# Spectral layer and two MLPs on one core: half sums and differences of the odd samples made by a negation and an in-place DMA add, with six x buffers and an earlier load

## Chip, core and metric

One core of one Trainium2 chip. The metric is the time of one execution on the device in microseconds, the median of the runs; lower is better. TensorE (PE) does the matrix products, VectorE (DVE), ScalarE (ACT) and GpSimd (POOL) the elementwise work, SyncE (SP) issues most DMAs; DMAs that add into their target are issued by GpSimd.

## What is computed

A spectral layer on x (2 batches, 3008 samples, 256 features), and two MLPs of width 2048 on its result. The change is in the forward transform of x.

```python
X = np.fft.rfft(x, axis=1)
Yr = Xr @ w_r - Xi @ w_i + b_r
Yi = Xr @ w_i + Xi @ w_r + b_i
Y = soft_threshold(Yr, 0.01) + 1j * soft_threshold(Yi, 0.01)
y = np.fft.irfft(Y, n=3008, axis=1)          # (2, 3008, 256)
h = y.reshape(6016, 256) @ w_in;  g = h * sigmoid(1.702 * h);  x1 = g @ w_out
h = x1 @ w_in2;                   g = h * sigmoid(h);          out = g @ w_out2
```

## The kernel before

The transform of 3008 samples is folded before TensorE sees it: samples are sorted into even (q = 0) and odd (q = 1), and of each kind the four that a symmetry ties together lie side by side in one row, so a tile `raw` has 128 rows of 4 x 256 numbers: two halves of 512 columns. A kind and batch (q, b) has three such tiles (j = 0, 1, 2). From each tile come the sum and the difference of its two halves (`halves`, line 313: 128x512 each; cs = 0 is the sum, cs = 1 the difference). For the even samples they are kept (`keep`) for use much later, for the odd ones they lie in `lv`. From these, `fold` makes the sum or difference of their own two 256-column halves (line 332, tile `xf`; for some of the odd ones first `dd` and then a second sum and difference of two `dd`, line 346). The `xf` tiles are the stationary operands of TensorE, which multiplies them with cosine and sine matrices (`m0`, loaded by `load_m`) into PSUM (`psf`); ScalarE copies the result out (line 446).

The forward stage works through 16 groups in one written order: groups 0 to 3 are the even samples of batches 0 and 1 (line 428, `fwd_pair`, two at a time), groups 4 to 7 the odd samples of batch 0 (t = 0 to 3), groups 8 to 11 the odd samples of batch 1, groups 12 to 15 the even samples again with other matrices (line 394, `fwd_mm`). t % 2 picks the half sums (t = 0, 2) or the half differences (t = 1, 3). In the loop over groups, `fold` runs three groups ahead of the products. A group of t < 2 has eight products of 190 columns; each product stands in the trace as two matmul records. The first product of such a group needs the first tile, the second product already the third tile.

Every engine runs its instructions in the written order (a region in which the scheduler is told to keep it), and SP and GpSimd issue their DMAs in that order too: an issue that waits holds up the ones behind it. Loads of x are issued on SP by `load_raw`; `raw` has three buffers, so a fourth tile waits until VectorE has read the first; the second batch's even x goes to other buffers (`xr`). `load_m` has four buffers, so the fifth matrix waits until TensorE is done with the first. After the forward transform, weights of the MLPs are converted in steps that are spread over the stages (lines 180 to 190: ScalarE, five VectorE operations, and a GpSimd DMA that adds in place, `cv_a<-cv_c`); the first such step stands on VectorE behind the folds of group 9.

Of the kernel before, what the change touches and what calls it, by code (L numbers as in the profile page):

```python
# [9 lines left out]
F32 = mybir.dt.float32  # L10
# [7 lines left out]
ALU = mybir.AluOpType  # L18

B, S, D, FF = 2, 3008, 256, 2048  # L20
HALF = S // 2
P = 128
NJ = 3
# [5 lines left out]
MW = 2 * NJ * CW  # L29
# [10 lines left out]
def split_sums(kind, q, p):  # L40
    return (kind, q) == ("f", 0) and CFG.get("eo", "1111")[p] == "1" or (kind, p) == ("i", 0) and CFG.get("eo", "1111")[2 + q] == "1"


def mshape(kind, q, p):
    if split_sums(kind, q, p):
        return 4, {("f", 0, 0): 190, ("f", 0, 1): 188, ("i", 0, 0): 192, ("i", 1, 0): 188}[kind, q, p]
    return {("f", 0, 0): (3, 380), ("f", 0, 1): (3, 376), ("f", 1, 0): (4, 190), ("f", 1, 1): (3, 376), ("i", 0, 0): (3, 378), ("i", 1, 0): (3, 376), ("i", 0, 1): (4, 190), ("i", 1, 1): (3, 376)}[kind, q, p]
# [9 lines left out]
def spectral_mlp_kernel(ctx, tc, xin, mfwd, minv, wc, bias, w_in1, w_out1, w_in2, w_out2, outT):  # L57
    nc = tc.nc
# [3 lines left out]
    def N(k):  # L62
        return CFG.get(k, NUM[k])

    def E(site, i=0):
        s = CFG.get(site, DEF[site])
        return {"V": nc.vector, "P": nc.gpsimd}[s[i % len(s)]]
# [15 lines left out]
    def opened(name, side=None, bufs=1, **kw):  # L83
        ex[name] = ExitStack()
        return ex[name].enter_context(tc.tile_pool(name=name, bufs=bufs, side=side, reuse_waits="tile", **kw))
# [5 lines left out]
    m_p = opened("m", "left", 4)  # L91
# [7 lines left out]
    def bank(i, name):  # L99
        return ps_p[i % 2].tile([P, 512], F32, tag="ps", name=name)  # L100
# [14 lines left out]
    def slot(cls, dtype, name):  # L115
        return xt_p.tile([P, 2 * D], dtype, tag=f"x{cls}", name=name, bufs=14 if cls == 0 else 12)
# [4 lines left out]
    def load_m():  # L121
        if not m_order:
            return
        kind, q, t = key = m_order.pop(0)
        nb, w = mshape(kind, q, t // 2)
        if kind == "f":
            m = m0_p.tile([P, NJ * 380], F32, tag="m0", name="m0")[:, : nb * w]
            m_tiles[key] = m.rearrange("p (j c) -> p j c", j=nb)
            src = mfwd[t // 2, q, t % 2][:, : nb * w]
            if key[1:] in ((0, 0), (0, 1)):  # L130
                return m_tiles[key], src.rearrange("p (j c) -> p j c", j=nb)
            nc.sync.dma_start(out=m, in_=src)
            return
        m = m_p.tile([P, MW], F32, tag="m", name="m")
        for cs in range(2):
            mc = m[:, cs * MW // 2 : cs * MW // 2 + nb * w]
            nc.sync.dma_start(out=mc, in_=minv[t // 2, q, cs][:, : nb * w])
            m_tiles[kind, q, t + cs] = mc.rearrange("p (j c) -> p j c", j=nb)
# [128 lines left out]
    def tick(k=1):  # L267
        window(k, settle(True))
        pump()
        cv_load(1 - len(loaded))  # L270
# [6 lines left out]
    region('fwd')  # L277

    m0_p = opened("m0", "left", 4)
    raw_p = opened("raw", "left", 3)  # L280
    lv_p = opened('lv', 'left', N('lvb'))
    xs_p = opened("xs", "left", 18)
    groups = [(0, b, cs) for b in range(B) for cs in range(2)]
    groups += [(1, b, t) for b in range(B) for t in range(4)]
# [1 line left out]
    held, kept = [], []  # L286
    raws, lvs, xs = {}, {}, {}
    raw_units = [(q, b, j) for q in range(2) for b in range(B) for j in range(NJ)]

    def load_raw(k=1):  # L290
        for _ in range(min(k, len(raw_units))):
            u = q, b, j = raw_units.pop(0)
            if (q, b) == (0, 1):
                raws[u] = [slot(h, F32, "xr")[:, :].rearrange("p (k d) -> p k d", k=2) for h in range(2)]
                for h in range(2):
                    nc.sync.dma_start(out=raws[u][h], in_=xin[q, b, j][:, 2 * h : 2 * h + 2])
                continue
            t = raw_p.tile([P, 4, D], F32, tag="raw", name="raw")
            raws[u] = t[:, 0:2], t[:, 2:4]
            nc.sync.dma_start(out=t, in_=xin[q, b, j])  # L300

    def halves(q, b, j, cs):
        if q == 0:
            if len(held) % 4 == 0:
                kept.append(m_p.tile([P, MW], F32, tag="m", name="keep"))
            k = len(held) % 4
            lv = kept[-1][:, k * 2 * D : (k + 1) * 2 * D].rearrange("p (k d) -> p k d", k=2)
            held.append(lv)
        else:
            lv = lv_p.tile([P, 2, D], F32, tag="lv", name="lv")  # L310
        lvs[q, b, cs, j] = lv
        r = raws[q, b, j]
        (nc.vector.tensor_sub if cs else nc.vector.tensor_add)(lv, *r)  # L313

    def fold(g):
        if g >= len(groups):
            return
        q, b, t = groups[g]

        cs, minus = t % 2, t in (1, 2)  # L320
        pair = []
        for j in range(NJ):
            if t == 0:
                halves(q, b, j, 0)
            lv = lvs[q, b, cs, j]
            e = E('dd', t * NJ + j) if g >= 2 else E('dd0', t * NJ + j)
            paired = q == 1 and t < 2 and j < 2
            if paired:
                xf = lv_p.tile([P, D], F32, tag="dd", name="dd", bufs=4)
            else:  # L330
                xf = xs_p.tile([P, D], F32, tag="xh", name="xf")
            (e.tensor_sub if minus else e.tensor_add)(xf, lv[:, 0], lv[:, 1])  # L332
            if t == 0:
                halves(q, b, j, 1)
                del raws[q, b, j]
                if (q, b) == (0, 0):
                    load_raw()
            if not paired:
                xs[(*groups[g], j)] = (xf, None)
                continue  # L340
            pair.append(xf)
            if j == 1:
                for x in range(2):
                    e = E('pr', 2 * t + x)
                    xf = xs_p.tile([P, D], F32, tag="xh", name="xf")
                    (e.tensor_sub if x else e.tensor_add)(xf, pair[0], pair[1])
                    xs[(*groups[g], x)] = (xf, None)

    def fold_pair(g):
        q, b, _ = groups[g]  # L350
        for j in range(NJ):
            for cs in range(2):
                halves(q, b, j, cs)
                xf = xs_p.tile([P, D], F32, tag="xh", name="xf")
                lv = lvs[q, b, cs, j]
                (nc.vector.tensor_sub if cs else nc.vector.tensor_add)(xf, lv[:, 0], lv[:, 1])
                xs[q, b, cs, j] = (xf, None)
            del raws[q, b, j]
            if b == 0:
                load_raw()  # L360

    def load_wc():
        raws["wc"] = raw_p.tile([P, 4, D], F32, tag="raw", name="wc_f")
# [55 lines left out]
    def fwd_pair(g):  # L419
        out = {}  # L420
        for h in (g, g + 1):
            out[h] = [bank(h, "psf") for _ in range(2)]
        for j in range(NJ):
            for h in (g, g + 1):
                q, b, t = groups[h]
                w = mshape("f", q, t // 2)[1]
                for mm in range(2):
                    nc.tensor.matmul(out[h][mm][:, :w], xs[q, b, t, j][0][:, mm * P : (mm + 1) * P], m_tiles["f", q, t][:, j, :w], start=j == 0, stop=j == NJ - 1)
        return [(h, out[h]) for h in (g, g + 1)]
# [51 lines left out]
    for j in range(NJ):  # L481
        load_raw()
        for ms, src in first:
            for k in ((0,), (1,), (2, 3) if split_sums("f", 0, 0) else (2,))[j]:
                nc.sync.dma_start(out=ms[:, k], in_=src[:, k])
    load_raw(3)
    fold_pair(0)
    load_m()
    fold_pair(2)
    load_m()  # L490
    xsp, lo_p = {}, []
    mids = [(b, p, j) for b in range(B) for p in range(2) for j in range(NJ)]

# [14 lines left out]
            xsp[b, p, j, cs, part] = t[:, :].rearrange("p (q m c) -> p q m c", q=2, m=2)  # L508

    prev = fwd_pair(0)  # L510
    fold(4)
    then = fwd_pair(2)
    load_m()
    fold(5)
    load_raw(3)
    for x in prev:
        fwd_evac(*x)
    load_m()
    fold(6)
    new_xt(1)  # L520
    pads(1)
    cv_load(1)
    prev = then
    for g, (q, b, t) in enumerate(groups):
        if g < 4:
            continue
        ps = fwd_mm(g)
        if b == B - 1 and m_order[0][0] == "f":
            load_m()
        fold(g + N('fa'))  # L530
        for x in prev:
            fwd_evac(*x)
        prev = [(g, ps)]
        if g == 6:
            wc_s = m_p.tile([P, MW], F32, tag="m", name="wc_s")[:, : 6 * D].rearrange("p (k d) -> p k d", k=2)
            load_wc()
        if g == 8:
            prep_wc()
            lo_p.append(wc_p)
        if g == 10:  # L540
            xsplit(N('n32'), 1)
        if g in N('tf'):
            tick(N('tf').count(g))
# [249 lines left out]
    prev = None  # L793
    for q in range(2):
        for b in range(B):
            for t in range(4):
# [5 lines left out]
                prev = (q, b, t, ps)  # L802
# [171 lines left out]
    for at, (l, i, p) in enumerate(seq):  # L974
# [8 lines left out]
        k = rate(at)  # L983
# [182 lines left out]
```

## Time and profile before

| | |
|---|---|
| median of 3 runs | 1153.8 us (1153.64 to 1153.8) |
| the profiled execution: its own time | 1153.61 us |
| its span, first to last instruction | 1151.8 us |
| TensorE busy | 1141.4 us |
| VectorE, ScalarE, GpSimd busy | 629.9, 775.1, 476.2 us |
| mean granted TensorE clock | 0.999 |

The times of rows are microseconds from the span's start in this one execution. A TensorE that is shown busy is not one at its peak, since matmuls are pipelined and their ends are modelled; starts are exact.

### The profile page before, as it was taken

Reading aid. Unit: us, or ns where it says so; the run is one execution under the profiler, and the core shown is the slowest. Engines: PE = TensorE matmul, PEld = TensorE weight load, DVE = VectorE, ACT = ScalarE, POOL = GpSimd, SP = SyncE. Lnnn points to the kernel's source line nnn. Section 1 sums busy time; section 2 is a strip of 40 time slices with the busy share of each in tenths; the row PEclk is TensorE's granted clock in tenths of the full one; section 3 lists DMA queues with packets and bytes.
Section 4 is the critical chain, followed back from the end, with each engine's and each line's share of the span. In section 5 each row is a group of like instructions: output and inputs, shape, how many; then the busy total and the mean of one; then the engine's idle time right before and its main releaser. Section 6 shows DMA issues by size and latency. Waiting matters only on the chain.

```text
span 1151.8 us, 14646 instructions
## 1 busy us (share of the span) xinstructions
PE 1141.4 (99%) x5094; PEld 947.1 (82%) x5094; DVE 629.9 (55%) x1014; ACT 775.1 (67%) x1446; POOL 476.2 (41%) x411
## 2 busy tenths in 40 slices
PE   9999999999999999999999999999999999999998
PEld 6768987878888888888889878888888888888897
DVE  8888997765565475564564642532622623623422
ACT  2587367877677676686677776766766866756755
POOL 0253164453444434444447645433343333333333
PEclk9999999999999999999999999999999999999999
DMA  8699493531121212212111100010000100100000
GB/s 312 168 185 240 113 160 79 109 81 37 49 61 37 72 39 55 56 38 73 46 47 37 46 26 3 1 38 1 19 19 1 37 1 1 37 1 1 37 1 32
DMA packets 39996, 68.95 MB, mean 60 GB/s; under 512 B 3697, under 2 KB 16241, under 8 KB 39922
## 3 DMA queue, kind: packets, MB, share of 16 engines
q1 hardware_dynamic: 26306, 45.51, 12.0%
q0 software_dynamic: 13616, 22.51, 11.5%
q8 instruction: 40, 0.66, 0.2%
q14 instruction: 34, 0.28, 0.1%
HBM read 35.15 MB, written 10.35 MB: 40 GB/s over the span
## 4 chain that ended last, share of the span: by engine, by line
PE 91%; DVE 3%; ACT 3%; issue 2%; DMA 2%; POOL 0%; SPq 0%; DVEq 0%; POOLq 0%; ACTq 0%
PE o L843 41%; PE x L871 36%; PE psm L575 5%; PE psi L394 4%; PE psf L394 3%; PE psm L572 1%; ACT yt L874 1%; DMA xr<-in_x 1%; DVE yt L893 0%; ACT x L782 0%; DMA raw<-in_wi 0%; ACT g L876 0%; ACT yt L890 0%; DVE keep L313 0%; DMA raw<-in_x 0%
## 5 line engine op out<-in xcount | busy, mean ns | idle before, releaser
L881 POOL TENSOR_TENSOR g<-yt,g 128x512 fp32r<-128x512 f32 (+1 forms) x282 | 362.8, 1298 | 495.9 <-PE x L871 359.8
L843 PE MATMUL o<-g,wo 128*128 128x512 f32 (+1 forms) x2304 | 560.0, 385 | 0.6 <-DMA wo<-cv_a 0.6
L871 PE MATMUL x<-x,wi 128*128 128x512 f32 (+1 forms) x2016 | 499.0, 386 | 3.4 <-ACT yt L912 2.1
L843 PEld LDWEIGHTS o<-g,wo 128*128 128x128 f32 x2304 | 432.4, 188 | 81.6 <-DMA wo<-cv_a 1.0
L871 PEld LDWEIGHTS x<-x,wi 128*128 128x128 f32 x2016 | 377.1, 188 | 80.0 <-ACT yt L912 5.0
L874 ACT ACTIVATE yt<-yt 128x512 f32<-128x512 f32 (+1 forms) x288 | 179.0, 622 | 253.7 <-DVE yt L922 204.9
L876 ACT CAST g<-yt 128x512 fp32r<-128x512 f32 (+1 forms) x384 | 235.2, 612 | 12.3
L922 DVE TENSOR_TENSOR yt<-yt,x 128x512 f32<-128x512 f32 (+1 forms) x96 | 64.7, 674 | 214.5 <-PE x L871 213.9
L893 DVE TENSOR_TENSOR yt<-yt,x 128x512 f32<-128x512 f32 (+1 forms) x96 | 64.8, 676 | 167.2 <-ACT yt L890 165.3
L881 DVE TENSOR_TENSOR g<-yt,g 128x512 fp32r<-128x512 f32 (+1 forms) x102 | 70.1, 687 | 73.5 <-ACT g L876 73.5
L190 POOL DMA_DIRECT2D cv_a<-cv_c x32 | 28.0, 876 | 111.8 <-DVE cv_c L189 105.7
L926 DVE TENSOR_TENSOR yt<-yt,x 128x512 f32<-128x512 f32 (+1 forms) x96 | 64.8, 675 | 0.0
L789 DVE TENSOR_TENSOR x<-yt,x 128x512 fp32r<-128x512 f32 (+1 forms) x44 | 46.4, 1054 | 29.5 <-ACT x L782 29.5
L910 ACT COPY yt<-x 128x512 f32<-128x512 f32 (+1 forms) x96 | 54.8, 571 | 3.3 <-PE x L871 3.3
L874 ACT ACTIVATE yt<-x 128x512 f32<-128x512 f32 (+1 forms) x96 | 56.1, 585 | 0.0
L912 ACT COPY yt<-x 128x512 f32<-128x512 f32 (+1 forms) x96 | 55.7, 580 | 0.1
L890 ACT COPY yt<-x 128x512 f32<-128x512 f32 (+1 forms) x96 | 54.6, 569 | 0.0
L394 PE MATMUL psi<-m,f 128*128 128x188 f32 (+3 forms) x224 | 45.1, 357 | 0.0
L394 PEld LDWEIGHTS psi<-m,f 128*128 128x128 f32 x224 | 37.6, 190 | 5.7
L394 PE MATMUL psf<-m,xf 128*128 128x190 f32 (+2 forms) x176 | 36.2, 367 | 1.0 <-DVE xf L332 0.6
L394 PEld LDWEIGHTS psf<-m,xf 128*128 128x128 f32 x176 | 29.6, 190 | 8.0 <-ACT xt L446 1.0
L782 ACT CAST x<-tmp 128x512 fp32r<-128x512 f32 (+1 forms) x36 | 22.1, 614 | 17.1 <-DVE tmp L791 15.5
(116 smaller groups left out, 839.4 us busy)
## 6 DMA issues: line engine op xcount, KB each, us to landing
raw<-in_wi SPq DMA_DIRECT2D x32, 256.0 KB, 3.7
cv_a<-cv_c POOLq DMA_DIRECT2D x32, 256.0 KB, 5.1
raw<-in_wo SPq DMA_DIRECT2D x16, 512.0 KB, 3.8
xl<-xt POOLq DMA_DIRECT2D x20, 256.0 KB, 7.9
out_t<-yt SPq DMA_DIRECT2D x20, 256.0 KB, 2.0
raw<-in_x SPq DMA_DIRECT2D x9, 512.0 KB, 5.8
wi<-tmp POOLq DMA_DIRECT2D x8, 256.0 KB, 4.8
w_in<-cv_a SPq DMA_DIRECT2D x8, 256.0 KB, 2.0
```

Of the source, the lines that this page charges most:

```text
L394: nc.tensor.matmul(ps, hi[:, c : c + P], m[:, k, :w], start=i == 0, stop=i == last)
L575: nc.tensor.matmul(t, st, mv, start=n == 0 and k == 0, stop=n == 3 and grp == 1 and k == 2)
L843: nc.tensor.matmul(acc[h, mm], st, mv, start=first and k == 0, stop=last and k == 2)
L871: nc.tensor.matmul(ps, st, mv, start=first and m == 0, stop=m == 2, skip_group_check=True)
L874: nc.scalar.activation(g, g if src is None else src, func)
L876: nc.scalar.copy(gh, g)
L881: eng.tensor_sub(gl, g, r32(gh))
L893: nc.vector.tensor_add(y1, y1, Y)
L910: nc.scalar.copy(y2, Z)
L912: nc.scalar.copy(y3, X)
L922: nc.vector.tensor_add(y2, y2, X)
L926: nc.vector.tensor_add(y3, y3, Z)
```

## The change

For the odd samples the two results no longer lie in tiles of their own but replace the two halves of the x tile itself. `second(b)` lets ScalarE negate the second half r1 in place. In batch 0, VectorE then makes the sum as r0 - (-r1) in place, and a GpSimd DMA reads the first half once more from DRAM and adds it to the negated half, which makes the difference. In batch 1 both results come from DMAs: one adds the second half to r0, one the first half to the negated r1. So of the 12 VectorE operations (128x512) three remain, and there are six ScalarE operations and nine adding DMAs of 256 KB that were not there. The x tiles get six buffers in place of three, and the loads of the second batch's odd x stand in the SP queue ahead of the third and fourth matrix. Copies out of groups 0 and 1 stand ahead of `fold(4)` in the text.

```diff
-    raw_p = opened("raw", "left", 3)
-    lv_p = opened('lv', 'left', N('lvb'))
+    raw_p = opened("raw", "left", 6)
+    lv_p = opened('lv', 'left', 4)
...
     def halves(q, b, j, cs):
-        if q == 0:
-            if len(held) % 4 == 0:
-                kept.append(m_p.tile([P, MW], F32, tag="m", name="keep"))
...
-        else:
-            lv = lv_p.tile([P, 2, D], F32, tag="lv", name="lv")
...
+    def second(b):
+        for j in range(NJ):
+            r = lvs[1, b, 0, j], lvs[1, b, 1, j] = raws.pop((1, b, j))
+            nc.scalar.mul(r[1], r[1], -1.0)
+            if b == 1:
+                for h in range(2):
+                    nc.gpsimd.dma_start(out=r[h], in_=xin[1, b, j][:, 2 - 2 * h : 4 - 2 * h], accum_op=ALU.add)
 
     def fold(g):
...
-            if t == 0:
-                halves(q, b, j, 0)
             lv = lvs[q, b, cs, j]
+            if (q, b, t) == (1, 0, 0):
+                r = lvs[q, b, 1, j]
+                nc.vector.tensor_sub(lv, lv, r)
+                nc.gpsimd.dma_start(out=r, in_=xin[q, b, j][:, 0:2], accum_op=ALU.add)
...
-            if t == 0:
-                halves(q, b, j, 1)
-                del raws[q, b, j]
-                if (q, b) == (0, 0):
-                    load_raw()
...
             del raws[q, b, j]
-            if b == 0:
-                load_raw()
...
+    load_raw(6)
+    load_m()
+    load_m()
     load_raw(3)
     fold_pair(0)
-    load_m()
     fold_pair(2)
-    load_m()
...
     prev = fwd_pair(0)
+    for x in prev:
+        fwd_evac(*x)
+    second(0)
     fold(4)
     then = fwd_pair(2)
     load_m()
     fold(5)
-    load_raw(3)
-    for x in prev:
-        fwd_evac(*x)
...
         for x in prev:
             fwd_evac(*x)
+        if g == 4:
+            second(1)
```

How it moves instructions, on three engines. First VectorE, from behind the last fold of group 3 on: the rows of groups 4 and 5 before. `lv<-raw` is a half sum or difference, the wait names what a row waits for (DMAHW: a load of SP has landed; DMASW: a DMA of GpSimd has landed).

```order
L313 TENSOR_TENSOR lv<-raw 128x512 [waits DMAHW7_49]
L332 TENSOR_TENSOR dd<-lv 128x256 [waits DVE_49]
L313 TENSOR_TENSOR lv<-raw 128x512
L313 TENSOR_TENSOR lv<-raw 128x512 [waits DMAHW0_49]
L332 TENSOR_TENSOR dd<-lv 128x256 [waits DVE_49]
L313 TENSOR_TENSOR lv<-raw 128x512
L346 TENSOR_TENSOR xf<-dd 128x256 [waits DVE_49]
L346 TENSOR_TENSOR xf<-dd 128x256
L313 TENSOR_TENSOR lv<-raw 128x512 [waits DMAHW1_49]
L332 TENSOR_TENSOR xf<-lv 128x256 [waits DVE_49]
L313 TENSOR_TENSOR lv<-raw 128x512
L332 TENSOR_TENSOR dd<-lv 128x256 x2
```

And the same place in the change, from behind its first half sum (`raw<-raw`, in place) to the last fold of group 5:

```order
L339 TENSOR_TENSOR dd<-raw 128x256 [waits DVE_49]
L331 TENSOR_TENSOR raw<-raw 128x512 [waits DMAHW0_49,Activation_49]
L339 TENSOR_TENSOR dd<-raw 128x256 [waits DVE_49]
L348 TENSOR_TENSOR xf<-dd 128x256 [waits DVE_49]
L348 TENSOR_TENSOR xf<-dd 128x256
L331 TENSOR_TENSOR raw<-raw 128x512 [waits DMAHW1_49,Activation_49]
L339 TENSOR_TENSOR xf<-raw 128x256 [waits DVE_49]
L339 TENSOR_TENSOR dd<-raw 128x256 [waits DMASW0_49]
L339 TENSOR_TENSOR dd<-raw 128x256 [waits DMASW1_49]
L348 TENSOR_TENSOR xf<-dd 128x256 [waits DVE_49]
L348 TENSOR_TENSOR xf<-dd 128x256
L339 TENSOR_TENSOR xf<-raw 128x256 [waits DMASW2_49]
```

Three half differences are gone from among the folds of group 4, and each fold of group 5 now waits for one adding DMA of GpSimd. The folds of groups 8 and 9 wait in the same way for the six of batch 1.

Second, GpSimd's queue from its last setting of `bias_f` on, as a piece of the difference:

```order
-L386 MEMSET xt_307 128x4x8
-L386 MEMSET xt_308 128x4x8
-L386 MEMSET xt_313 128x4x8
-L386 MEMSET xt_314 128x4x8
+L332 DMA raw<-in_x 128x512 x3
+L386 MEMSET xt_304 128x4x8
+L386 MEMSET xt_305 128x4x8
+L386 MEMSET xt_310 128x4x8
+L386 MEMSET xt_311 128x4x8
+L318 DMA raw<-in_x 128x512 x6
```

Nine DMAs have come in, in one queue, ahead of the first weight's DMA; nothing stood there before.

Third, SP's queue of loads behind the second batch's even x, as a piece of the difference (`m_265` and `m_280` are the third matrix of the odd samples, `m_295` and `m_292` the fourth, `raw_319` and `raw_316` a weight):

```order
-L132 DMA m_188<-in_mf 128x760
-L132 DMA m_209<-in_mf 128x760
-L132 DMA m_265<-in_mf 128x1128
+L132 DMA m_168<-in_mf 128x760
+L132 DMA m_170<-in_mf 128x760
 L300 DMA raw<-in_x 128x1024 x3
-L132 DMA m_295<-in_mf 128x1128
-L162 DMA raw_319<-in_wi 128x2x128
-L163 DMA raw_319<-in_wi 128x2x128
+L132 DMA m_280<-in_mf 128x1128
+L132 DMA m_292<-in_mf 128x1128
```

The three loads of the second batch's odd x have moved ahead of the third matrix, which waits for TensorE.

## Rows read from the trace of the kernel before

**Rows 1.** The page: busy time of the engines, share of the span, instructions.
```profile
PE 1141.4 (99%) x5094; PEld 947.1 (82%) x5094; DVE 629.9 (55%) x1014; ACT 775.1 (67%) x1446; POOL 476.2 (41%) x411
```

**Rows 2.** Timeline of TensorE, 0 to 110 us: start, length, what, [idle before <-releaser].
```profile
22.84 0.56 PE L394 MATMUL psf<-m,xf 128*128 128x190 f32 x2 [0.38 <-DVE xf L346]
24.03 35.62 PE L394 MATMUL psf<-m,xf 128*128 128x190 f32 x174 [0.63 <-DVE xf L332]
```

**Rows 3.** Chain that ended last, 0 to 60 us: start, length, what.
```profile
6.03 6.32 DMA xr<-in_x
...
12.45 0.70 DVE keep L313
...
22.92 0.61 DVE lv L313
```

**Rows 4.** TensorE's waits, whole span: us in total, times, longest.
```profile
PE x L871 <- ACT yt L912: 2.1, 5, 1.0
...
PE x L871 <- DVE yt L922: 0.8, 1, 0.8
...
PE o L843 <- DMA wo<-cv_a: 0.6, 1, 0.6
```

**Rows 5.** TensorE's groups by shape, 20 to 60 us: busy, mean ns | idle before.
```profile
L394 PE MATMUL psf<-m,xf 128*128 128x376 f32 x48 | 15.5, 479 | 0.0
...
L394 PE MATMUL psf<-m,xf 128*128 128x188 f32 x64 | 10.3, 322 | 0.0
```

**Rows 6.** Timeline of VectorE, 0 to 110 us.
```profile
18.84 0.69 DVE L313 TENSOR_TENSOR lv<-raw 128x512 f32<-128x512 f32 x1
...
22.16 0.75 DVE L346 TENSOR_TENSOR xf<-dd 128x256 f32<-128x256 f32 x2
...
35.91 0.42 DVE L185 TENSOR_SCALAR cv_c<-cv_c 128x512 f32<-128x512 f32 x1
...
38.02 0.70 DVE L189 SCALAR_TENSOR_TENSOR cv_c<-raw,cv_c 128x512 f32<-128x512 uint32 x1
```

**Rows 7.** ScalarE's groups, 12 to 42 us.
```profile
L446 ACT COPY xt<-psf 128x128 f32<-128x128 f32 (+2 forms) x58 | 11.5, 279 | 23.9 <-PE psf L428 16.0 <-PE psf L394 7.6
...
L370 ACT ACTIVATE wc_s<-wc_f 128x512 f32<-128x512 f32 x1 | 0.7, 650 | 0.0
```

**Rows 8.** Timeline of SP's queue, 0 to 70 us.
```profile
12.37 9.17 SPq L132 DMA_DIRECT2D m<-in_mf  x3
21.65 3.29 SPq L300 DMA_DIRECT2D raw<-in_x  x3
```

**Rows 9.** Stretches: busy PE, PEld, DVE, ACT, POOL, PEclk, DMA share, GB/s.
```profile
20.00:22.00 2.00, 2.00 (x8) 1.14 (x6) 1.97 (x4) 1.35 (x7) 0.00 (x0) 1.00 0.01 3
22.00:24.00 2.00, 1.01 (x4) 0.30 (x2) 1.97 (x6) 1.05 (x6) 0.00 (x0) 1.00 0.92 276
24.00:26.00 2.00, 1.97 (x12) 1.97 (x13) 1.97 (x6) 0.60 (x3) 0.00 (x0) 1.00 0.97 347
```

**Rows 10.** Timeline of GpSimd, 0 to 60 us.
```profile
39.04 1.00 POOL L190 DMA_DIRECT2D cv_a<-cv_c  x1 [37.37 <-DVE cv_c L189]
```

**Rows 11.** DMAs of 139 to 144.6 us: KB each, median us from issue to landing.
```profile
wi<-tmp POOLq DMA_DIRECT2D x1, 256.0 KB, 3.3
```

**Rows 12.** DMAs of 39 to 46 us.
```profile
cv_a<-cv_c POOLq DMA_DIRECT2D x1, 256.0 KB, 5.8
```

**Rows 13.** DMA queues, 12 to 18 us: packets, MB, share of 16 engines.
```profile
q1 hardware_dynamic: 922, 2.50, 103.9%
```

**Rows 14.** DMA queues, 101 to 104 us.
```profile
q0 software_dynamic: 334, 0.61, 112.8%
```

**Rows 15.** DMA queues, 98 to 99.5 us.
```profile
q0 software_dynamic: 92, 0.16, 56.3%
q1 hardware_dynamic: 95, 0.28, 51.2%
```

**Rows 16.** TensorE's groups, 0 to 8 us.
```profile
L472 PE MATMUL warm<-ones_f 128*128 128x128 f32 x26 | 5.9, 427 | 1.1 <-DVE neglam L474 1.1
```

More of the change, by code (lines that the diff above doesn't have):

```diff
@@ L302, in halves @@
     def halves(q, b, j, cs):
-        if q == 0:
-            if len(held) % 4 == 0:
-                kept.append(m_p.tile([P, MW], F32, tag="m", name="keep"))
-            k = len(held) % 4
-            lv = kept[-1][:, k * 2 * D : (k + 1) * 2 * D].rearrange("p (k d) -> p k d", k=2)
-            held.append(lv)
-        else:
-            lv = lv_p.tile([P, 2, D], F32, tag="lv", name="lv")
+        if len(held) % 4 == 0:
+            kept.append(m_p.tile([P, MW], F32, tag="m", name="keep"))
+        k = len(held) % 4
+        lv = kept[-1][:, k * 2 * D : (k + 1) * 2 * D].rearrange("p (k d) -> p k d", k=2)
+        held.append(lv)
         lvs[q, b, cs, j] = lv
@@ L328, in fold @@
             if paired:
-                xf = lv_p.tile([P, D], F32, tag="dd", name="dd", bufs=4)
+                xf = lv_p.tile([P, D], F32, tag="dd", name="dd")
             else:
```

## The prediction

> **What bounds the kernel.** The page comes first: TensorE is busy for 1141.4 of 1151.8 us [rows 1], so all that any change can take away by waiting less is 10.4 us. The timeline of TensorE shows how little of that lies where this change acts: from 24.03 us on, 174 matmul records of the forward stage follow one another for 35.62 us with no idle time, and ahead of them stand two waits of 0.38 and 0.63 us, both for VectorE's `xf` [rows 2]. The chain says who is late before: loads of x until 12.35, then VectorE alone, keep and lv and their folds, until TensorE takes over [rows 3]. So VectorE bounds group 4's start, and nothing behind it up to 59.65. The other waits of TensorE, 2.1, 0.8 and 0.6 us [rows 4], are in the MLPs, on work that the change doesn't touch.
>
> That gives the ceiling. A record of 188 or 190 columns costs 10.3/64 = 0.161 us [rows 5]. Groups 4 and 5 have 32; two ran at 22.84, the other 30 from 24.03 end at 28.9. Without either wait the 32 would run from 22.84 - 0.38 = 22.46 and end at 27.6. **The change can win 1.3 us here**, 0.1%. About 0.2%, 2.3 us, is what a measurement of this kernel can tell from no change.
>
> **VectorE.** Nine of the twelve half operations, 0.69 us each [rows 6], go: about 6 us. Of these only the three ahead of group 4's last fold lie on the path. The in-place sums begin as lv did, at 18.84. The pair of folds ended at 22.16 + 0.75 = 22.91; two halves of some 0.65 (with overlap) fewer, 21.6. The third sum then ends at 22.3, its fold at 22.8. Group 4's first product can start at 22.46, the second, which needs that fold, at 22.9, and its last 14 records end at 25.2. Before, group 4 ended at 24.03 + 14 x 0.161 = 26.3. So VectorE's relief is worth 1.1 us, if the next group is ready.
>
> **ScalarE.** Six negations, nearest row 0.65 us (128x512) [rows 7], 3.9 us. Three come behind the copies of groups 0 and 1, three behind those of 2 and 3, where ScalarE idled 16.0 us on TensorE [rows 7]. Cost: nothing, and if that cover were gone 3.9 us of ScalarE, which TensorE sees only once a PSUM buffer is late.
>
> **Loads.** The three matrices took 9.17 us to issue, the third held until TensorE was done with the first; the three loads of x (0.52 MB each) came at 21.65 [rows 8]. DMA was still from 20 to 22 (share 0.01) and full from 22 on [rows 9]. In the change those loads can be issued some 8 us sooner: their new buffers were last read before 12.45 [rows 3]. So the lull fills: 1.57 MB run from about 20 on, then the two matrices (1.15 MB) and a weight (0.52 MB). By itself this costs and gains nothing, since x of batch 1 was not waited for. But it puts the loads beside the adding DMAs.
>
> **The adding DMAs of batch 0.** The first half sum ends at 18.84 + 0.69 = 19.53. From a VectorE operation's end to GpSimd's issue passed 0.32 us (38.02 + 0.70 [rows 6] to 39.04 [rows 10]), so the first is issued at 19.85 and the third at 22.3 + 0.3 = 22.6. Group 5's second product needs the third. No row shows one that reads DRAM. The nearest are the same size from SBUF: 3.3 us to landing with nothing else running [rows 11], 5.8 us for one that stood beside a weight's and a matrix's loads [rows 12].
>
> Rates tell why. Loads alone moved 2.50 MB in 6 us, 0.417 MB/us [rows 13]; adding DMAs alone 0.61 MB in 3 us, 0.203 MB/us, 1.29 us for 256 KB (0.262 MB) [rows 14]; the two together 0.16 and 0.28 MB in 1.5 us [rows 15], so 0.107 MB/us for the adding ones: 2.45 us each. What an adding DMA takes beside its data is 3.3 - 1.29 = 2.0 us. The three land, one behind the other in one queue:
> - alone: 22.6 + 3.3 = 25.9;
> - shared: 19.85 + 2.0 + 3 x 2.45 = 29.2. The loads have enough to share with: 3.24 MB from 20 on, of which these 9 us move some 2 MB;
> - last: if loads go first, 20 + 3.24/0.417 = 27.8, then 3 x 1.29: 31.7.
>
> I take 29.2, because the loads of the change are then in full run; 5.8 us after the issue, 28.4, is not far. The fold takes 0.45, the handover 0.1, and 14 records 2.25: group 5 ends at 29.2 + 2.8 = 32.0 where it ended at 28.9: **+3.1 us**, bounds -0.2 (alone) and +5.6 (last). The 1.1 us of VectorE's relief is in this.
>
> By the Trainium skill ("DMA: Bandwidth & Descriptors", Anatomy of one DMA), a DMA of GpSimd takes 2.0 us plus its bytes at 436 GB/s, here an estimate of 2.6 us. By that the third would land at 25.2, group 5 end at 28.0, and the sum would be -0.9 us. The trace doesn't bear it out for DMAs that add: 3.3 us alone, 5.8 beside loads.
>
> **The six of batch 1.** They follow in the same queue, and groups 8 and 9 wait for them. Groups 6 and 7 have 24 records of 376 columns, 15.5/48 = 0.32 us [rows 5], 7.7 us, and their sums and differences are there. So group 8 starts at 39.7, its second product at 40.0. Shared all the way, from 21.85 on, the eighth DMA (the last sum) ends at 21.85 + 8 x 2.45 = 41.45, its fold at 41.9: a wait of 1.9 us. The ninth ends at 43.9, its fold at 44.35, and group 9's second product would come at 44.5: no wait. Behind that fold stands the first weight step on VectorE, 35.91 to 38.72, 2.8 us [rows 6], ahead of group 10's folds: ready at 47.6, while group 9 ends at 46.75: 0.9 us. If instead each kind runs at its rate alone, all loads (with the complex weights, 3.77 MB) and nine adding DMAs need 9.0 + 11.6 = 20.6 us from 20 on, the eighth is in at 39.3, and neither wait is there. So 0 to 2.8 us; I take the middle, **+1.4**. Later the weight steps run some 8 us late on VectorE, TensorE some 5; TensorE meets no other wait up to 59.65 [rows 2] that they could lengthen, and their products are used over 100 us later.
>
> **Sum.** 3.1 + 1.4 = 4.5 us. The profiled execution took 1153.61 us, its span and 1.8 around it; with 4.5 it would take 1158.1. The median of the runs is 0.2 above it, so I say **1158.3 us**.
>
> **Rivals.**
> - *The adding DMAs land as if alone* (not slower). For it: they come one by one, and each engine's share may go to them first. Against it: the loads that the change itself moves to 20 to 28 us. Group 5 then ends at 28.7, -0.2 us: 1153.6 us; with the 5.8 us of the row beside loads +2.3. It decides at a landing of 26.1, 3.5 us behind the third issue; at that the change is even. The skill's 2.6 us stands on its side.
> - *The clock falls while TensorE waits.* Between group 4's end at 25.2 and 29.7 TensorE would do one product, where its longest wait until now was 1.0 us [rows 4], with the granted clock at 1.00 around the early waits [rows 9]. At the start, 26 records of 128 columns took 5.9 us [rows 16], 1.77 ns a column against 0.86 later: the lower level, 1.2 GHz. If that many microseconds came back at half rate, 3 us more: 1161.3. No row here shows a fall behind a wait of this length. The skill ("TensorE: Matmul & The Clock Gate", the HAM clock gate) says that an idle TensorE falls back to 1.2 GHz; no run here shows it.
> - *The second set is the bound.* If the complex weights' load and the weights keep sharing longer than counted, or SP's earlier loads slow the sums too, groups 8 to 10 wait 4 us or more in place of 1.4: 1161.
> - *Faster by over 0.2%.* The 1.3 us of the ceiling are not enough; the 3.5 us of waits in the MLPs would have to shrink too, to 1149 at best. Nothing in the change reaches them.
>
> **Numbers.** Chances: my forecast (1156 to 1160.5) 0.55; as if alone, or nearly, 0.22; the clock 0.13; the second set 0.06; faster 0.04. The range of 1154.5 to 1161.8 leaves out the faster case, the lower half of the second, and the dearer parts of clock and second set, some 0.2. Faster 0.04, same 0.22, slower 0.74.
>
> **What will show it.** Right: the wait ahead of group 4 shrinks to 0.4 us or less; a new wait of 3 to 6 us behind group 4, ended by VectorE's `xf`, which itself waited for `raw<-in_x` of GpSimd; those DMAs show 5 to 9 us to landing; DMA share is full from 20 to 40 us; from group 6 on a smaller wait at most. Wrong: landing in under 4 us and no wait behind group 4; or the granted clock at half behind it; or the largest new wait at group 8; or a difference that arises behind 60 us.

## The result, and the profile after

The change made the kernel slower: 1161.6 us (median of 4 runs, 1161.35 to 1162.8) against 1153.8 (4 runs, 1153.64 to 1153.93), ratio 1.007, interval 1.0052 to 1.0087. The difference is 7.8 us where the prediction had 4.5. The profiled execution took 1162.8 us, the slowest of the four, with a span of 1160.8; it is 9.2 us above the profiled execution of before.

The page's busy line, against [rows 1]: TensorE is busy for 1.3 us more, so most of the loss is waiting.

```profile
PE 1142.7 (98%) x5094; PEld 947.6 (82%) x5094; DVE 625.8 (54%) x1005; ACT 779.5 (67%) x1452; POOL 484.2 (42%) x420
```

TensorE's timeline from 22 us on, which answers to [rows 2]:

```profile
22.31 0.48 PE L394 MATMUL psf<-m,xf 128*128 128x190 f32 x2
23.40 2.53 PE L394 MATMUL psf<-m,xf 128*128 128x190 f32 x14 [0.60 <-DVE xf L339]
32.56 35.20 PE L394 MATMUL psf<-m,xf 128*128 128x190 f32 x160 [6.63 <-DVE xf L348]
67.59 3.60 PE L575 MATMUL psm<-wc_s,xt 128*128 128x512 f32 x8
```

The wait of 0.38 us ahead of group 4 is gone, the 0.63 has become 0.60, and a wait of 6.63 us has come between groups 4 and 5. All three are waits for VectorE's `xf`. Behind the last, 160 records run without idle time: none at groups 8 to 10. The waits of [rows 4] are there about as before, 2.4 (2.1 before), 0.8 and 0.6 us in the MLPs. VectorE's timeline, against [rows 6], and GpSimd's, against [rows 10], show who it was:

```profile
19.28 0.69 DVE L331 TENSOR_TENSOR raw<-raw 128x512 f32<-128x512 f32 x1
...
22.92 0.42 DVE L339 TENSOR_TENSOR xf<-raw 128x256 f32<-128x256 f32 x1
28.23 0.43 DVE L339 TENSOR_TENSOR dd<-raw 128x256 f32<-128x256 f32 x1 [4.89 <-DMA raw<-in_x]
31.09 0.43 DVE L339 TENSOR_TENSOR dd<-raw 128x256 f32<-128x256 f32 x1 [2.42 <-DMA raw<-in_x]
31.55 0.76 DVE L348 TENSOR_TENSOR xf<-dd 128x256 f32<-128x256 f32 x2
32.97 2.44 DVE L339 TENSOR_TENSOR xf<-raw 128x256 f32<-128x256 f32 x7 [0.66 <-DMA raw<-in_x]
...
44.39 0.42 DVE L185 TENSOR_SCALAR cv_c<-cv_c 128x512 f32<-128x512 f32 x1
```
```profile
20.29 1.93 POOL L332 DMA_DIRECT2D raw<-in_x  x2 [18.86 <-DVE raw L331]
23.18 0.86 POOL L332 DMA_DIRECT2D raw<-in_x  x1 [0.97 <-DVE raw L331]
...
23.96 5.65 POOL L318 DMA_DIRECT2D raw<-in_x  x6
```

The folds of group 5 start at 28.23, 31.09 and 32.97, each when its adding DMA has landed; the last was issued at 23.18. Group 5's first product needs the pair of folds behind the second DMA, which ends at 31.55 + 0.76 = 32.31; its second product, two records on, needs the third DMA, which landed at 32.94. What the DMA queues moved in the meantime, 22.3 to 32.9 us (packets, MB, share of 16 engines):

```profile
q0 software_dynamic: 599, 1.10, 60.3%
q1 hardware_dynamic: 633, 1.72, 46.7%
```

The adding DMAs (q0) moved 1.10 MB beside 1.72 MB of loads. The three of batch 0 are 0.79 MB of that; the other 0.31 belongs to the six queued behind them. The stretches, against [rows 9], show a second thing (the sixth number is the granted clock, the seventh the DMA share):

```profile
26.00:28.00 2.00, 0.00 (x0) 0.00 (x0) 0.00 (x0) 0.56 (x3) 2.00 (x4) 1.00 1.08 265
28.00:30.00 2.00, 0.00 (x0) 0.00 (x0) 0.43 (x1) 0.00 (x0) 1.59 (x2) 0.81 1.04 262
30.00:32.00 2.00, 0.00 (x0) 0.00 (x0) 0.88 (x3) 0.00 (x0) 0.00 (x0) 0.50 1.11 238
...
34.00:36.00 2.00, 2.00 (x8) 2.00 (x7) 1.74 (x6) 0.25 (x2) 0.00 (x0) 0.50 1.12 233
36.00:38.00 2.00, 2.00 (x11) 1.66 (x10) 0.00 (x0) 0.95 (x6) 0.00 (x0) 0.98 1.13 214
```

TensorE did nothing from 25.9 on. In 28 to 30 the granted clock falls, and it stays at 0.50, the level of 1.2 GHz, up to 36, with TensorE at work again from 32.56. How long the fall lasts differs: in a second profile of the change the clock was at 0.50 up to 38, and the 160 records took 36.39 us:

```profile
32.94 36.39 PE L394 MATMUL psf<-m,xf 128*128 128x190 f32 x160 [6.50 <-DVE xf L348]
```

**The sum of the profiled execution.** TensorE's first product of the next stage starts at 67.59; before, its forward records ended at 59.65 [rows 2] and that product stood at 59.49 (a modelled end overlaps). So 8.1 us have arisen by then, all of it before group 6's first product, and from there to the last output the two traces run in parallel within 0.23 us. The end of the span adds 0.66 us (below), the time around the span 0.2: 9.2.

### The profile page after: what moved, and what is told of

The parts are those of the page before. It is cut to its first block, busy times and chain, and to the rows that moved or that the text cites. A ratio compares the mean times of both kernels' runs of the same rounds, so it can differ in the third digit from the quotient of the medians.

```text
span 1160.8 us, 14666 instructions
## 1 busy us (share of the span) xinstructions
PE 1142.7 (98%) x5094; PEld 947.6 (82%) x5094; DVE 625.8 (54%) x1005; ACT 779.5 (67%) x1452; POOL 484.2 (42%) x420
## 4 chain that ended last, share of the span: by engine, by line
PE 92%; DMA 2%; ACT 2%; issue 1%; DVE 1%; POOL 0%; SPq 0%; POOLq 0%; DVEq 0%
PE o L846 42%; PE x L874 37%; PE psm L578 5%; PE psi L394 4%; PE psf L394 3%; DMA raw<-in_x 1%; PE psm L575 1%; ACT yt L877 1%; DMA m<-in_mf 1%; ACT x L785 0%; DVE yt L896 0%; DMA wo<-cv_a 0%; DVE x L792 0%; ACT yt L893 0%; PE psm L581 0%
```

## The experiments

Theory: batch 0's adding DMAs land late because they share the DMA engines with the loads, and the clock falls behind the wait. Rivals were tried one by one. Kernels of one comparison ran on one chip with the kernel before. One thing shifts profiled executions against each other, whatever the edit: VectorE's first half sum of the odd samples starts at 19.28 us in the change, at 19.80 in its second profile and at 18.82 with the wait filled, which is the same program up to there; in the kernel before it starts at 18.84, in the delay alone, again the same up to there, at 19.86.

**All on VectorE.** The change without adding DMAs and negation; the early load and the six buffers stay.

```diff
+                if t == 0:
+                    nc.vector.tensor_add(r[0], r[0], r[1])
+                else:
+                    nc.vector.scalar_tensor_tensor(out=r[1], in0=r[1], scalar=-2.0, in1=r[0], op0=ALU.mult, op1=ALU.add)
-            nc.scalar.mul(r[1], r[1], -1.0)
-            if b == 1:
-                for h in range(2):
-                    nc.gpsimd.dma_start(out=r[h], in_=xin[1, b, j][:, 2 - 2 * h : 4 - 2 * h], accum_op=ALU.add)
```

> No adding DMA and no negation: VectorE makes the half sums and differences of both batches of odd samples in place, the sums ahead of group 4 (8), the differences only among the folds of group 5 (9) as r0+r1 - 2*r1. Six buffers and the earlier load stay as in the change. Theory 'adding DMAs' (the loss comes from group 5 waiting for three adding DMAs that land 8 to 10 us after their issue, plus the clock that falls in that wait): no wait behind group 4, granted clock 1.00 throughout, the 1.1 us of VectorE's relief ahead of group 4 is kept: 1152.5 to 1153.5 us. Rival 'load order' (the earlier load of the second batch's x itself costs, since it delays matrices and weights): 1155 us or more with a wait at group 6 or 7 for a matrix.

Measured: 1155.3 us (10 runs, 1153.76 to 1157.21), ratio 1.001 (1.0001 to 1.002). TensorE and VectorE:

```profile
26.48 0.56 PE L395 MATMUL psf<-m,xf 128*128 128x190 f32 x2 [0.59 <-ACT xt L447]
27.34 22.85 PE L395 MATMUL psf<-m,xf 128*128 128x190 f32 x94 [0.30 <-DVE xf L340]
```
```profile
25.46 0.76 DVE L349 TENSOR_TENSOR xf<-dd 128x256 f32<-128x256 f32 x2
...
26.86 2.44 DVE L340 TENSOR_TENSOR xf<-raw 128x256 f32<-128x256 f32 x7
```

The 1 us of gain did not come. Group 4's last 14 records start at 23.36, 0.67 us earlier than before [rows 2], but the three differences that stood ahead of it now stand ahead of group 5, which waits 0.59 and 0.30 us. The first wait stands under ScalarE's name, but it ends 0.26 us behind VectorE's pair of folds (25.46 + 0.76 = 26.22), as the wait in the change ends 0.25 us behind its pair (32.31 and 32.56); the third record waits for VectorE's `xf` of 26.86. What VectorE saves at one group it owes at the next. The time is that of before within 0.2%, so the early load and the buffers cost next to nothing, and the loss of the change is in its DMAs and negations. The negations alone were not run; they do not hold up group 4, whose last 14 records start 4.12 us behind the first half sum in the change (19.28 to 23.40) and 4.11 here, without them.

**Batch 0 on VectorE.** Only batch 1 with negation and adding DMAs; batch 0 has the two operations of the kernel above.

```diff
+            if q == 1 and b in (0,) and t < 2:
...
-            nc.scalar.mul(r[1], r[1], -1.0)
             if b == 1:
+                nc.scalar.mul(r[1], r[1], -1.0)
```

> Batch 0 as in the run with all on VectorE, batch 1 by negation and six adding DMAs as in the change. Theory 'adding DMAs of batch 0': the six now start with an empty queue of their own, share with the loads until about 30 us, land by 38 us, before groups 8 and 9 need them at 35 and 37.5 us or just after: 1152.5 to 1155 us. Rival 'adding DMAs of batch 1 cost as well': a wait of 2 to 5 us at group 8 or 9, 1155 to 1159 us, clock perhaps fallen there.

Measured: 1156.9 us (10 runs, 1155.65 to 1159.03), ratio 1.002 (1.0011 to 1.003). This is above what was expected. Its forward stage in the profile ends 1.0 us later than before, 0.3 more than with all on VectorE; the rest arises behind it. No wait is listed at groups 8 to 10, but the last 158 records take 33.60 us where they took 33.03 with all on VectorE, and that 0.5 us arises at groups 8 and 9. Besides, VectorE is late: the operation that stands at 120.92 before stands at 123.96, 3.0 us later, where TensorE is 1.0 late; at 174.18 TensorE has a wait that was not there. Before, and here:

```profile
120.92 1.28 DVE L611 TENSOR_TENSOR f<-th 128x512 f32<-128x512 f32 x2
```
```profile
123.96 1.29 DVE L616 TENSOR_TENSOR f<-th 128x512 f32<-128x512 f32 x2
```
```profile
174.18 0.96 PE L876 MATMUL x<-x,wi 128*128 128x512 f32 x3 [0.20 <-ACT eo L708]
```

Of the adding DMAs, issued from 22.66 on, the queues show in 22.4 to 26.5 us nothing but loads. Why the adding ones moved nothing for some 4 us stays open: in the change, those issued from 20.29 on moved 0.16 MB in 22 to 24 us beside 0.47 MB of loads.

```profile
q1 hardware_dynamic: 509, 1.67, 102.6%
```

**The loads late.** The change with the three loads of x back behind the third matrix.

```diff
-    load_raw(3)
     fold_pair(0)
...
     fold(5)
+    load_raw(3)
```

> The change, but the three loads of the second batch's odd x stand behind the third matrix again, so they are issued at about 21.6 us. Theory 'shared with the loads': batch 0's three adding DMAs start in the lull of 20 to 22 us; the first lands in about 5 us, the third in 5 to 7 in place of 9.8; the wait ahead of group 5 falls from 6.6 to 2 to 4 us and the clock doesn't fall; but batch 1's sums can only start when the late loads land, 28 to 31 us, so a wait at group 8: 1156 to 1160 us. Rival 'an adding DMA that reads DRAM takes 8 us or more by itself': the wait stays at 6 us or more, 1161 us or more.

Measured: 1164.5 us (4 runs, 1162.71 to 1165.97), ratio 1.0085 (1.0067 to 1.0103). A miss: it got worse, with waits of 5.66 and 0.63 us at group 5 where 2 to 4 was expected. The first adding DMA, issued at 20.86 into the lull, the only one in the stretch 20 to 21.5, has landed after 4.1 us (row of DMA issues: count, KB each, us to landing); and TensorE:

```profile
raw<-in_x POOLq DMA_DIRECT2D x1, 256.0 KB, 4.1
```
```profile
32.15 0.97 PE L394 MATMUL psf<-m,xf 128*128 128x190 f32 x2 [5.66 <-DVE xf L348]
```

So an adding DMA that reads DRAM need not take 8 us. But the next two fell among the loads that now started at 22.2, and took 8.7 and 9.5 us. Moving the loads moves the collision, it doesn't remove it.

**The wait filled.** The change with 30 products on a constant tile between groups 4 and 5, which nothing reads.

```diff
+        if g == 5:
+            warm = bank(5, "warm")
+            for _ in range(30):
+                nc.tensor.matmul(warm[:, :P], ones_f, ones_f, start=True, stop=True)
         ps = fwd_mm(g)
```

> The change, with 30 products of 128 columns on a constant tile between groups 4 and 5 on TensorE, some 6.4 us, into a PSUM bank that nothing reads: they fill the wait and change no result. Theory 'clock': the granted clock stays at 1.00, group 5 and the start of group 6 run at 0.16 us a record from the start, 1.7 us less than the change: 1159.5 to 1160.2 us. Rival 'the clock costs nothing because groups 5 and 6 wait for VectorE anyway': same as the change within 0.4 us, 1161.6.

Measured: 1162.5 us (4 runs, 1162.19 to 1163.0), ratio 1.0068 (1.0053 to 1.0083).

```profile
25.30 6.86 PE L531 MATMUL warm<-ones_f 128*128 128x128 f32 x60
32.00 33.50 PE L394 MATMUL psf<-m,xf 128*128 128x190 f32 x160
...
175.41 4.06 PE L394 MATMUL psi<-m,f 128*128 128x376 f32 x12 [0.46 <-DVE rt L730]
179.66 0.96 PE L878 MATMUL x<-x,wi 128*128 128x512 f32 x3 [0.19 <-ACT eo L710]
```

The granted clock stays at 1.00 in all stretches from 24 to 38, and the 160 records take 33.50 us in place of 35.20: the fall costs 1.7 us. The forward stage ends 2.3 us sooner than in the change, 0.5 of it because VectorE's first half sum started at 18.82 and not 19.28. But the total, expected at 1159.5 to 1160.2, doesn't fall: at 175 to 180 us TensorE meets new waits. So the price of the fall is shown for these records, and not in the time of the kernel.

**No loads beside.** The third and fourth matrix of the odd samples are not loaded (GpSimd sets their tiles to 0.01), and the first weight is loaded behind the complex weights. GpSimd's two settings stand ahead of the six adding DMAs of batch 1, which are so issued from 25.92 on in place of 23.96.

```diff
+            if key[1:] in ((1, 2), (1, 3)):
+                nc.gpsimd.memset(m, 0.01)
+            else:
+                nc.sync.dma_start(out=m, in_=src)
-            nc.sync.dma_start(out=m, in_=src)
...
-    cv_load(1)
...
             load_wc()
+            cv_load(1)
```

> The change, but nothing is loaded beside batch 0's adding DMAs: the third and fourth matrix of the odd samples are not loaded (GpSimd sets their tiles to 0.01 in their place, behind the third adding DMA, so the products of groups 6, 7, 10 and 11 have wrong values, at the same shapes and counts), and the first weight is loaded behind the complex weights. Theory (the adding DMAs are slow because loads share the DMA engines): once the early loads of x are in, some 24.7, the adding ones go at 1.29 us each; the third, issued near 23.2, lands before 28.5 (5 us or less instead of 9.8), the wait ahead of group 5 is 1 to 2.5 us instead of 6.6, the granted clock stays at 1.0, and the forward stage ends 2 to 3.5 us later than before instead of 8.1. Rival (an adding DMA that reads DRAM is slow behind others of its kind, whoever else loads): the third lands at 31 or later, the wait is 5 us or more and the clock falls. The total is not the point, since the weights come later: 1154.5 to 1158 by the theory.

Measured: 1160.2 us (4 runs, 1158.23 to 1161.81), ratio 1.0052 (1.0035 to 1.0068). TensorE, VectorE, the three DMAs and the stretches:

```profile
28.91 35.17 PE L397 MATMUL psf<-m,xf 128*128 128x190 f32 x160 [2.98 <-DVE xf L351]
```
```profile
26.18 0.42 DVE L342 TENSOR_TENSOR dd<-raw 128x256 f32<-128x256 f32 x1 [2.83 <-DMA raw<-in_x]
27.44 0.42 DVE L342 TENSOR_TENSOR dd<-raw 128x256 f32<-128x256 f32 x1 [0.84 <-DMA raw<-in_x]
...
28.68 2.44 DVE L342 TENSOR_TENSOR xf<-raw 128x256 f32<-128x256 f32 x7
```
```profile
raw<-in_x POOLq DMA_DIRECT2D x3, 256.0 KB, 5.9
```
```profile
28.00:30.00 2.00, 1.09 (x6) 1.12 (x7) 1.97 (x6) 0.00 (x0) 2.00 (x5) 0.92 1.06 170
30.00:32.00 2.00, 2.00 (x8) 2.00 (x7) 1.46 (x5) 0.60 (x3) 1.57 (x2) 0.50 0.98 143
```

The DMAs now land some 1.25 us apart (26.18, 27.44, 28.68 for the folds), the 1.29 us that the prediction worked out for 256 KB alone; the third lands at 28.66, 5.5 us behind its issue (the theory said 28.5 and 5). That is 4.3 us sooner than in the change's profile. Most of it goes to the loads, not all: the six behind had moved some 0.1 MB by then, where in the change they had moved 0.31. The forward stage ends 4.4 us later than before, not 2 to 3.5, and the time is above the 1154.5 to 1158 expected. The wait is 2.98 us, half a microsecond over what was expected, and the clock fell all the same, which was not: 0.50 in 30 to 32, when TensorE was at work again from 28.91.

**Batch 1 on VectorE.** Batch 0's three adding DMAs alone; batch 1 in place on VectorE, as above.

```diff
+            if q == 1 and b in (1,) and t < 2:
...
-            nc.scalar.mul(r[1], r[1], -1.0)
-            if b == 1:
-                for h in range(2):
-                    nc.gpsimd.dma_start(out=r[h], in_=xin[1, b, j][:, 2 - 2 * h : 4 - 2 * h], accum_op=ALU.add)
+            if b == 0:
+                nc.scalar.mul(r[1], r[1], -1.0)
```

> The change with adding DMAs for batch 0 alone; batch 1's sums and differences are made in place on VectorE, with no negation. Theory (batch 0's three DMAs cost everything, the six behind them nothing): the three land as in the change, 28 to 33, the wait ahead of group 5 is 6 to 7 us, the clock falls, the forward stage ends 8 us later than before, and the time is that of the change, 1160.5 to 1162. By the prediction's own sum, with its term for batch 1, the time would be 1.4 us under the change. A third way: the six DMAs that are queued behind slow the first three through the shared engines; then the wait here is 5 us or less and the time 1159 or less.

Measured: 1161.6 us (4 runs, 1160.54 to 1162.69), ratio 1.0068 (1.0051 to 1.0085); the change itself, in the same comparison, 1162.1 (1161.58 to 1164.33), ratio 1.0073 (1.0058 to 1.0088):

> The change itself, unaltered, on the same chip as the other three. Both theories: 1161 to 1162.5, third adding DMA of batch 0 in at 32.5 to 33.5, the granted clock at half behind it.

Without the six, 22.3 to 31.5 us, and TensorE:

```profile
q1 hardware_dynamic: 873, 2.05, 59.3%
q0 software_dynamic: 432, 0.79, 46.5%
```
```profile
30.90 35.48 PE L401 MATMUL psf<-m,xf 128*128 128x190 f32 x160 [5.39 <-DVE xf L355]
```

The third lands at 31.35 in place of 32.94 (33.23 in the change's second profile), but it was also issued sooner, at 22.77 in place of 23.18 and 23.70. From its issue it took 8.6 us without the six, and with them 9.8, 9.5 and, with the wait filled, 9.2: the six behind it cost it 0.7 to 1.2 us, since they take engine time before it is done. The wait is 5.4, between the first and the third way expected. In time the two kernels can't be told apart. VectorE is in step here: the operation of 120.92 stands at 127.57, 6.65 us later, and TensorE is 6.7 late. So of the third's way from issue to landing the two experiments give about 1 us to the six behind, and up to 4.3 to the loads, with a part of the six's in it; a kernel without both wasn't run.

**The delay alone.** To see whether VectorE's lateness made the new waits of the filled wait: the kernel before with 26 such products between groups 4 and 5, no DMA that adds.

> The kernel before, with 26 products of 128 columns on a constant tile between groups 4 and 5 (at 0.229 us each, measured in the filled wait, 5.95 us): TensorE is late by about as much as in the experiment with the filled wait, 5.8 us, but no DMA adds and VectorE is on time. Theory (what that experiment lost again near 175 us came from VectorE, whose weight steps the adding DMAs held up more than TensorE): the forward stage ends 5.5 to 6 us later, no new wait comes near 175 us, and the time is 1159.3 to 1159.9. Rival (any delay of TensorE of this size costs more behind it): 1161 or more, with the same waits near 175 us.

Measured: 1160.5 us (4 runs, 1159.73 to 1161.32), ratio 1.0055 (1.004 to 1.007). The forward stage came 6.8 us later, not 5.9, because VectorE's first half sum started 1.0 us later in this execution (19.86 for 18.84), which is ahead of the edit; the 26 products themselves cost 5.8. VectorE is as late as TensorE and no more, and yet TensorE loses 0.5 us at 180 us. So neither way expected came as it was put. VectorE's timeline and the DMA that it waits for, here and then before, name the reason:

```profile
160.91 0.55 DVE L726 TENSOR_TENSOR ac<-rt,psi 128x377 f32<-128x377 f32 x1 [1.07 <-DMA yt<-ac]
```
```profile
yt<-ac POOLq DMA_DIRECT2D x1, 188.0 KB, 6.6
```
```profile
153.27 0.55 DVE L722 TENSOR_TENSOR ac<-rt,psi 128x377 f32<-128x377 f32 x1 [0.25 <-DMA yt<-ac]
```
```profile
yt<-ac POOLq DMA_DIRECT2D x1, 188.0 KB, 5.2
```

In the inverse stage VectorE waits for a GpSimd DMA that frees `ac`: 0.25 us before, 0.24 in the change, 1.07 here, 0.89 with the filled wait. TensorE follows a little later. Why it lands later in some executions stays open, and with it some of the scatter of the medians.

With the filled wait a second thing is added, and there the theory holds. The operation of 120.92 stands 7.8 us later, TensorE's products 5.85; with batch 0 on VectorE it is 3.0 and 1.0, with no loads beside 7.7 and 4.4, but 6.65 and 6.7 with batch 1 on VectorE, and 8.0 and 8.1 in the change. So the six DMAs of batch 1 hold VectorE, their folds and the weight steps behind them, some 2 to 3 us more than TensorE, unless TensorE itself is held by batch 0's. VectorE has 1.0 us of idle time behind it, at 130.79 before, so some 0.9 is left in the inverse stage (2.2 with no loads beside); there TensorE has none, and with the filled wait it is 7.0 us late behind 172 instead of 5.85: about 1.2 us for VectorE's lag and the DMA together. Another 0.6 is lost at 243 to 251 us of before, where TensorE waits for `yt`; what stands behind that was not followed. What the clock gives back is paid there.

**GpSimd in place of VectorE.** A try at a version that beats both: the kernel before, with the half differences as plain subtractions on GpSimd.

```diff
-        (nc.vector.tensor_sub if cs else nc.vector.tensor_add)(lv, *r)
+        (nc.gpsimd.tensor_sub if q == 1 and b == 0 and cs else nc.vector.tensor_sub if cs else nc.vector.tensor_add)(lv, *r)
```

> The kernel before, with batch 0's three half differences of the odd samples made by GpSimd as plain subtractions (1.32 us each by its rows of the same shape) in place of VectorE: no negation, no adding DMA, loads and buffers as before. Theory (the gain that the change was after is VectorE's relief ahead of group 4, worth 1.0 us of waits there, and only the adding DMAs spoil it): the three differences lie beside VectorE's work and are there before group 5 wants them, the waits of 0.38 and 0.63 us ahead of group 4 shrink to 0 to 0.6 together, none comes at group 5, and the time is 0.4 to 1.3 us under before. Rival (VectorE and GpSimd hinder each other in SBUF, so that VectorE's operations of 13 to 24 us get longer): the waits stay or grow, and the time is that of before or up to 1 us above it.

> The same with the half differences of both batches on GpSimd. Batch 1's were not waited for, so by the theory nothing is added: 0.4 to 1.3 us under before, within 0.3 us of the kernel with batch 0's alone. Rival: three more operations of GpSimd at 25 to 33 us, beside VectorE's folds, cost time there: a wait at groups 8 or 9 and more than 0.5 us above its sister.

Measured: 1157.2 us (11 runs, 1155.77 to 1158.16), ratio 1.0019 (1.001 to 1.0028); with both batches 1157.7 (11 runs, 1155.6 to 1159.4), ratio 1.0021 (1.0011 to 1.003), before 1154.4 here. The rival was right on the cause and short on the size: 2.2 us by the ratio where it had up to 1. The two versions can't be told apart in time. GpSimd's three, and VectorE at that time:

```profile
16.34 4.34 POOL L313 TENSOR_TENSOR lv<-raw 128x512 f32<-128x512 f32 x3 [14.91 <-DMA raw<-in_x]
```
```profile
16.38 1.51 DVE L356 TENSOR_TENSOR xf<-keep 128x256 f32<-128x256 f32 x1
17.81 1.75 DVE L313 TENSOR_TENSOR keep<-xr 128x512 f32<-128x512 f32 x1
19.60 1.37 DVE L356 TENSOR_TENSOR xf<-keep 128x256 f32<-128x256 f32 x1
```
```profile
24.87 0.56 PE L394 MATMUL psf<-m,xf 128*128 128x190 f32 x2 [1.02 <-DVE xf L346]
```

While GpSimd subtracts, VectorE's sum of 0.42 us takes 1.4 to 1.5 and one of 0.69 takes 1.75: it loses 3.1 us on three operations, to save three of 0.69, and TensorE's waits grow: 1.02 us ahead of group 4, where it was 0.38 [rows 2], and 1.53 new ahead of that. In the profile with both batches the granted clock fell as well, though TensorE's waits were short, 1.44, 1.03 and 0.63 us, and the 174 records took 37.29 us in place of 35.61; in the profile with batch 0 alone, with waits of 1.53, 1.02 and 0.63, it didn't fall:

```profile
26.70 37.29 PE L394 MATMUL psf<-m,xf 128*128 128x190 f32 x174 [0.63 <-DVE xf L332]
```
```profile
28.00:30.00 2.00, 2.00 (x8) 2.00 (x7) 2.00 (x7) 0.60 (x3) 0.67 (x1) 0.50 0.90 330
```

No version here beats the kernel before.

## Why the prediction was right in sign and short in size

The step that failed is the size of one term, the adding DMAs of batch 0 ("shared: 29.2", +3.1 us): the third landed at 32.94, later even than the bound "last" of 31.7, and group 5 began 6.2 us late. The second failure is that the forecast put the clock at nothing behind that wait; its fall cost 1.7 us and more. The +1.4 for batch 1, which never came, hid a part of both: that 1161.6 lies as near to 1158.3 as it does is partly luck. One of the prediction's own signs of being wrong came (the granted clock at half), and of its signs of being right the wait (6.63 for 3 to 6) and the landing (7.9 to 9.8 for 5 to 9) were exceeded; 0.9 us of the difference arose behind 60 us, which it had named as a sign of being wrong too.

- **What bounds the place, and the ceiling.** VectorE bounded group 4's start. The 1.1 us of relief came whole: from the first half sum to group 4's last 14 records it is 4.12 us in the change (19.28 to 23.40) and 5.19 before (18.84 to 24.03). In this execution 0.6 of it shows, since the first half sum stood 0.44 us later, which differs from one execution to the next.
- **ScalarE's negations at nothing:** no wait of TensorE names them.
- **The adding DMAs of batch 0, which decide.** The mechanism was right: loads beside, a full DMA share from 20 to 40 us, the wait behind group 4 ended by `xf`, that by `raw<-in_x`, which took 7.9 to 9.8 us. The size failed: "shared: 29.2" against 32.94, 3.7 us. The run with batch 1 on VectorE is the case that the term describes, three DMAs beside the loads with nothing behind them, issued from 19.88 on (counted: 19.85). There the third landed at 31.35, 2.1 us too late. Nothing of them moved up to 22.8, 2.9 us behind the issue, and then 0.79 MB took 8.3 us, 0.095 MB/us: the 2.0 us beside the data, taken from a DMA with nothing else running, and the 0.107 MB/us, from 1.5 us of one row, were both too good. The six behind, left out by "one behind the other in one queue", moved 0.31 MB before the third was in and cost 0.7 to 1.2 us. The later issue adds 0.4. Group 5 begins 6.2 us late where it was to end 3.1 late.
- **The clock, put down as a rival at 0.13 and 3 us,** came true beside the forecast and not in its place. Its 3 us doesn't come out of its own words: 4.5 us at half rate lose 2.25. Filling the wait measures the fall: 1.7 us over the 160 records, and 2.9 in the change's second profile. By the Trainium skill ("TensorE: Matmul & The Clock Gate", the HAM clock gate) an idle TensorE falls to 1.2 GHz; the trace agrees, 0.50 behind the wait of 6.63 us. The error of the prediction was to let a long wait and a full clock stand together in one case.
- **The six of batch 1, +1.4: nothing.** The last two landed about as counted: 41.99 and 43.23 for 41.45 and 43.9. But TensorE came to them 5 us later, because of the first wait. Two waits on one path were added where the first one covers the second. The weight step on VectorE came 8.5 us later, as said; that TensorE meets no other wait which it could lengthen was read up to 59.65 only, and is wrong for the inverse stage: in the kernels where TensorE is less late than VectorE, it pays 0.5 to 2.0 us there.
- **As if alone,** the main rival, needed the third at 26.1. An adding DMA in the lull took 4.1 us, 0.6 above the 3.5 that this needed; the third of three with early loads and the later six beside, 5.5. The 2.6 us that the prediction estimated from the Trainium skill ("DMA: Bandwidth & Descriptors", Anatomy of one DMA) is met by none of 256 KB in the kernel before: 3.3 us at best [rows 11].
- **Not in the sum:** 0.66 us at the end of the span, which no part of the sum looked at, told below.

For the profiled execution: 0.6 of relief, against some 6.8 of waiting, 1.9 within group 5's products (the lag of TensorE grows from 6.2 to 8.1 there: 1.7 by the clock, the rest by the third DMA's fold), 0.2 later, 0.7 at the end, 0.2 around the span: 9.2.

## What to carry to other kernels

Before an operation is moved from a busy engine to a DMA, work out when that DMA lands with everything that is queued with it, ahead of it, beside it and behind it; here 0.69 us on VectorE became 8 to 10 us of latency at a place with no slack. A wait of several microseconds on TensorE is to be counted with a fall of its clock behind it, here 1.7 to 2.9 us, and waits on one path are not added: the first covers what would have come next. And relief counts only if the next consumer doesn't ask for the same work one group later.

## What the runs showed of the hardware

- Adding DMAs of one GpSimd queue overlap: later ones take engine time while an earlier one is still under way (0.31 MB before the third of nine was in, which landed 0.7 to 1.2 us later for it).
- The granted clock fell behind a wait of 2.98 us too, and in one execution behind waits of 1.44, 1.03 and 0.63 us; both times the fall showed when TensorE was already at work again.
- Each adding DMA makes the end of the program longer. From the end of the last output's issue on SP to the end of the span (1151.8, 1154.2, 1158.8 and 1160.8 us for none, six, three and nine) it took 3.4 us before, 3.9 with six more such DMAs, 3.7 with three and 4.1 with nine, some 0.07 us each. All twelve profiles fit: 3.4 to 3.5 in the five without such DMAs, 4.1 in the five with nine. SP's last rows, of before and of the change:

```profile
1146.37 1.99 SPq L849 DMA_DIRECT2D out_t<-yt  x4
```
```profile
1155.21 1.49 SPq L852 DMA_DIRECT2D out_t<-yt  x3
```

- VectorE's additions and subtractions of two float32 tensors took 2.5 to 3.6 times as long while GpSimd made such a subtraction: 1.51 us against 0.42, 1.75 against 0.69.
